# Attention and a token mixer on one core: masks of all pairs from batch 1 on added by VectorE, with the scale and the minus sign taken into the masked block

## The chip, the cores and the metric

The kernel runs on one core of a Trainium2 chip. The metric is the device time of one execution in microseconds; a time given for a kernel is the median of its runs. One further execution is taken with the hardware profiler, and every row of a profile shown here comes from such an execution. The engines are called TensorE (PE in the rows; PEld is its weight load), VectorE (DVE), ScalarE (ACT), GpSimd (POOL) and SyncE (SP), whose queue issues the transfers.

## The reference

Batch 8, 8 heads, 576 positions, head dimension 64, model width 512, everything in fp32.

```python
scores = q @ k.T / sqrt(64)                       # per batch and head, 576 x 576
rel    = pos[:, None] - pos[None, :]
plain  = (rel >= 0) & (rel < 32)                  # heads 0 to 3
dil    = (rel >= 0) & (rel < 128) & (rel % 4 == 0)  # heads 4 to 7
scores = where(mask, scores, -1e9);  scores -= max(scores)
attn   = exp(scores) / (sum(exp(scores)) + 1e-9)
x      = concat_heads(attn @ v)                   # 8 x 576 x 512
theta  = x @ w_theta
y      = w_tok_r @ (x * cos(theta)) + w_tok_i @ (x * sin(theta))
u      = x + y
out    = u + relu(u @ w_ch)
```

The host puts the positions of the dilated heads in order of their remainder by 4, so that both masks become a window of 32 positions inside its own stretch. A block of 32 queries then needs 64 keys.

## The kernel before

**The work.** Heads go in pairs, (batch, pair) with pair 0 to 3. For one pair nine blocks of 128 partitions (two heads, two strips of 32 queries) by 64 keys are computed (`scores`, line 547) into PSUM banks of the kind "s", of which there are two: one for blocks 0 to 4, one for blocks 5 to 8. The mask is an additive tile `mskb` of zeros and large negative numbers. It is added in one of two ways, which `on_pe(b, pr)` chooses:

- *On TensorE* (batch 0 and the pairs (1,2), (1,3), (2,0) and (2,1)): a matmul of an identity with the mask opens the accumulation in the bank (`mask_on_pe`, L501) and the scores are added to it. VectorE takes the maximum over the bank (`row_max`, L507) and, from batch 1 on, multiplies it by minus an eighth (L515). ScalarE computes exp(scale x score + bias) from PSUM, block by block, with its sum (L565); the bank is given back only then.
- *On VectorE* (all other pairs): the matmuls start the accumulation themselves. One instruction per block (`mask_scores`, L486) adds the mask, writes the sum to SBUF (tile `P`) and keeps the maximum; the bank is given back after it. VectorE multiplies the nine maxima by minus an eighth (L578), and ScalarE computes the exponentials from SBUF in place (L584).

Both ways end alike: the sums are inverted (L587, L588), GpSimd multiplies the exponentials by them (L590), VectorE transposes the blocks (`turn`, L608, eight per pair), TensorE multiplies them with the values (`pv`, L704; the tile va holds keys of blocks 0 to 4, vb those of blocks 5 to 8, vb has one buffer), and ScalarE copies the outcome to x (L664). x is then rounded into `xh` and its rest (L678 to L684), `theta` multiplies it with w_theta (L776, L781), cosine and sine follow (L1302 to L1316 and the transposed tail at L858 and L867), `z` is their product with x (L735, L737), the token mix is `token` (L1373) for batches 0 and 1 and a form with seven products in place of eight (`fast_step`, L1169) from batch 2 on, and `chan` (L1406) multiplies with w_ch. The residuals are L1346 and L1382. In the start-up the weights are unpacked and split as well (st_wtk, st_wch: L400 to L427), and the combined token weights of the seven-product form are built by GpSimd, VectorE and ScalarE (tx, ta to td) and stored (tw_t, L1100).

**The order.** Each engine runs its instructions in the order of the program. The program is written by a planner, the class `Order`: every piece of work is a generator that says before each step which engine it needs and for how long (`yield "DVE", 145 * (g1 - g0)`), or what it waits for. The planner keeps the time at which each engine would be free by these costs and lets the step with the lowest rank start. So a changed cost or a step on another engine reorders everything that is planned beside it, on all engines and on the transfer queue. The start-up (batch 0, the scores of batch 1 and of the pairs (2,0) and (2,1), theta of batch 1) is planned by the ranks of a table; from the token mix of batch 1 on, `steady()` gives TensorE a fixed order, and the others follow due times from it.

## Time and profile before

| | us |
|---|---|
| median of 3 runs (lowest, highest) | 564.9 (564.89, 566.3) |
| the profiled execution | 562.37 |
| its span, first to last instruction | 560.6 |
| TensorE busy / mean granted clock | 530.9 / 0.991 |
| VectorE busy | 434.9 |
| ScalarE busy | 372.4 |
| GpSimd busy | 332.5 |

A row of groups reads: line, engine, operation, output <- inputs with shapes, number of instructions, busy time, mean ns of one, idle time of the engine ahead of them and what ended it. A row of a timeline reads: start, duration, engine, line, operation, and in brackets the idle time ahead of it with the instruction that ended it; x5 at its end means five of a kind together, which overlap. A row of waits reads: who waited for whom, us in total, times, longest. "128*64" in a matmul's row is the part of the array that it uses. L12 is line 12 of the kernel.

### The profile page before, as it was taken

What the parts mean: (1) busy time and instruction counts of PE and PEld (TensorE: products, weight loads), DVE (VectorE), ACT (ScalarE), POOL (GpSimd) and SP (SyncE); (2) the same over time, 40 slices, a digit from 0 to 9 for tenths busy, and PEclk for the clock granted to TensorE, in tenths of its full rate; (3) what the DMA queues carried; (4) which work ended last, traced back from release to release, by engine and by line L of the source; (5) the groups of instructions that cost most, each with busy time, mean ns of one, the idle gap of its engine ahead of it and who ended that gap; (6) DMA issues with size and microseconds to landing.
All of it is one profiled execution on the core that took longest, in us unless ns stands there. A gap on an engine that the chain in (4) does not pass through costs nothing.

```text
span 560.6 us, 14386 instructions
## 1 busy us (share of the span) xinstructions
PE 530.9 (95%) x5320; PEld 481.5 (86%) x5320; DVE 434.9 (78%) x1315; ACT 372.4 (66%) x1033; POOL 332.5 (59%) x351
## 2 busy tenths in 40 slices
PE   4897799889998999999999999999999999999997
PEld 3744689778997899998999899998999899989997
DVE  3889799994687787979897997979797997748322
ACT  1598966868748578487776778487767767567220
POOL 2228858788994274763567374655476375727660
PEclk9999799899999999999999999999999999999999
DMA  8991535832659948995499918993599817690622
GB/s 303 400 390 29 177 108 185 256 118 96 201 200 309 317 162 324 322 263 189 141 363 292 307 44 314 324 279 149 199 341 290 276 63 227 213 279 37 211 92 85
DMA packets 59126, 124.41 MB, mean 222 GB/s; under 512 B 5424, under 2 KB 24624, under 8 KB 58800
## 3 DMA queue, kind: packets, MB, share of 16 engines
q1 hardware_dynamic: 59056, 123.49, 64.8%
q8 instruction: 42, 0.69, 0.5%
q14 instruction: 28, 0.23, 0.1%
HBM read 99.88 MB, written 23.59 MB: 220 GB/s over the span
## 4 chain that ended last, share of the span: by engine, by line
PE 70%; DVE 9%; DMA 9%; POOL 5%; ACT 4%; issue 2%; SPq 1%; DVEq 0%; POOLq 0%
PE c L1406 16%; PE th L776 12%; PE C L1169 9%; PE D L1169 7%; PE A L1169 5%; PE B L1169 4%; PE s L547 4%; PE o L704 4%; PE y L1373 4%; DMA vb<-in_vw_dram 4%; DMA st_wtk<-in_wtk_dram 3%; DVE pt L608 3%; POOL z L737 1%; DMA first_k<-in_kT_dram 1%; PE th L781 1%
## 5 line engine op out<-in xcount | busy, mean ns | idle before, releaser
L608 DVE STREAM_TRANSPOSE pt<-P 32x288 f32<-32x288 f32 x224 | 105.2, 470 | 11.8 <-POOL P L590 7.3
L1406 PE MATMUL c<-u,late_wc 128*128 128x288 f32 x768 | 108.3, 295 | 0.0
L1406 PEld LDWEIGHTS c<-u,late_wc 128*128 128x128 f32 x768 | 105.6, 188 | 2.6
L584 ACT ACTIVATE P<-P,mx 128x64 f32<-128x64 f32 x216 | 72.3, 336 | 12.7 <-DVE mx L578 12.5
L776 PE MATMUL th<-wthh,xh 128*128 128x512 f32 x224 | 74.9, 395 | 0.0
L590 POOL TENSOR_TENSOR P<-P,sm 128x576 f32<-128x576 f32 x32 | 39.5, 1235 | 59.0 <-DVE mx L578 29.4
L1187 POOL TENSOR_TENSOR u<-x,u 128x288 fp32r<-128x288 f32 x48 | 40.1, 838 | 20.8 <-ACT u L1185 20.6
L1185 ACT CAST u<-x 128x288 fp32r<-128x288 f32 x48 | 20.5, 427 | 45.0 <-DVE x L1195 45.0
L776 PEld LDWEIGHTS th<-wthh,xh 128*128 128x128 f32 x224 | 42.1, 188 | 9.2
L776 PE MATMUL th<-wthl,xh 128*128 128x512 f32 x112 | 44.3, 396 | 0.0
L486 DVE CUSTOM_DVE_ANT_0 P<-s,mskb 128x64 f32<-128x64 f32 x216 | 33.2, 217 | 14.3 <-PE s L547 14.3
L584 ACT ACTIVATION_READ_ACCUMULATOR P<-P,mx 128x1 f32 x216 | 40.4, 187 | 0.0
L664 ACT COPY x<-o 128x576 f32<-128x576 f32 x32 | 29.5, 921 | 15.0 <-PE o L704 14.9
L737 POOL TENSOR_TENSOR zl<-g,zh 128x512 fp32r<-128x512 f32 x7 | 9.1, 1297 | 48.9 <-ACT zh L735 48.9
L1382 DVE SCALAR_TENSOR_TENSOR x<-c,x 128x288 f32<-128x288 f32 x64 | 28.3, 449 | 12.3 <-PE c L1406 12.2
L547 PE MATMUL s<-k,q 128*64 128x64 f32 x1008 | 36.6, 226 | 0.0
L547 PEld LDWEIGHTS s<-k,q 128*64 128x64 f32 x1008 | 32.8, 140 | 3.7 <-issue 2.7
L704 PEld LDWEIGHTS o<-pt,va 128*64 128x64 f32 x600 | 21.4, 140 | 7.2 <-issue 4.9
L949 POOL TENSOR_TENSOR s<-f,x 128x256 f32<-128x256 f32 x24 | 17.8, 740 | 16.1 <-DVE f L937 13.7
L704 PE MATMUL o<-pt,va 128*64 128x64 f32 x600 | 25.6, 230 | 1.7 <-ACT pt L622 1.2
L1373 PE MATMUL y<-wt_g,z 128*128 128x288 f32 x96 | 20.7, 320 | 6.7 <-POOL z L737 4.1
L776 PEld LDWEIGHTS th<-wthl,xh 128*128 128x128 f32 x112 | 21.0, 188 | 4.0
(245 smaller groups left out, 1609.4 us busy)
## 6 DMA issues: line engine op xcount, KB each, us to landing
q<-in_qT_dram SPq DMA_DIRECT2D x32, 576.0 KB, 5.8
late_wt_a<-tw_t SPq DMA_DIRECT2D x24, 576.0 KB, 6.2
wt_g<-tw_b SPq DMA_DIRECT2D x22, 576.0 KB, 6.1
va<-in_vw_dram SPq DMA_DIRECT2D x30, 320.0 KB, 5.6
k<-in_kT_dram SPq DMA_DIRECT2D x28, 304.0 KB, 6.0
out_dram<-x SPq DMA_DIRECT2D x28, 288.0 KB, 2.1
vb<-in_vw_dram SPq DMA_DIRECT2D x29, 256.0 KB, 4.5
xd<-xq SPq DMA_DIRECT2D x24, 288.0 KB, 5.3
```

Source lines behind the costliest of these rows:

```text
L486: pin(nc.vector.tensor_tensor_reduce(out=P[:, n], in0=ps[:, n - g0], in1=mskb[:, mask_of(pr, n)], op0=ALU.add, op1=ALU.max, scale=1.0, sca ...
L547: pe(nc.tensor.matmul(ps[64 * e:64 * e + 64, n - g0], q[:, qb], k[:, QB * qb:QB * qb + BW], start=not masked, stop=not masked or n == g1 - 1))
L584: table(nc.scalar.activation(P[:, n], P[:, n], AF.Exp, bias=mx[:, n:n + 1], scale=SCALE, accum_out=sm[:, n:n + 1]))
L590: pin(nc.gpsimd.tensor_tensor(P, P, sm.unsqueeze(2).to_broadcast([128, NJ, BW]), op=ALU.mult))
L608: pin(nc.vector.transpose(pmats[b, pr][k0:k0 + QB, :, hh, QB * e:QB * e + QB], P[p0:p0 + QB, :, QB * o:QB * o + QB]))
L664: pin(nc.scalar.copy(dst, src))
L704: pe(nc.tensor.matmul(ps[64 * hh:64 * hh + 64, BW * j:BW * j + BW], v[:, 64 * hh:64 * hh + 64], pmats[b, pr][:, j, hh], start=True, stop=T ...
L776: pe(nc.tensor.matmul(pt, l, r, start=(n == 0), stop=(n == 3 * NC - 1)))
L1169: pe(nc.tensor.matmul(ps, l, r, start=first and n == 1, stop=last and n == 3 * len(ks), skip_group_check=more))
L1187: pin(nc.gpsimd.tensor_tensor(ul[b, d][:, ts], x[:, ts], uh[b, d][:, ts].bitcast(F32), op=ALU.subtract))
L1373: pe(nc.tensor.matmul(ps, l[:, cs], r, start=(n == 0), stop=(n == 3 * NK - 1)))
L1406: pe(nc.tensor.matmul(ps, l[:, cs], r[:, ts], start=(n == 0), stop=(n == 3 * NC - 1)))
```

## The change

Two edits. First, the masked block is no longer plain score plus mask with a running maximum: it is scaled by minus an eighth, and its minimum is kept. Minus an eighth times the maximum is the minimum of the scaled values, so the kept value is the bias of the exponentials, the multiplication L578 goes (24 times), and the exponentials take a scale of minus one. Second, `on_pe` is true for batch 0 alone: the pairs (1,2), (1,3), (2,0) and (2,1) get their masks on VectorE, as all later pairs have them. L501, L507, L515 and L565 run for batch 0 alone or, as L515 and L565, not at all. From line 578 on the changed kernel's lines have numbers lower by 2 (L608 becomes L606, L704 becomes L702, L1373 becomes L1371).

```diff
--- before.py
+++ after.py
@@ -485,12 +485,12 @@
         for n in range(g0, g1):
             pin(nc.vector.tensor_tensor_reduce(
                 out=P[:, n], in0=ps[:, n - g0], in1=mskb[:, mask_of(pr, n)],
-                op0=ALU.add, op1=ALU.max, scale=1.0, scalar=-3e38, accum_out=mx[:, n:n + 1]))
+                op0=ALU.add, op1=ALU.min, scale=-SCALE, scalar=3e38, accum_out=mx[:, n:n + 1]))
         give(*rel)
         signal(key)
 
     def on_pe(b, pr):
-        return b == 0 or (b, pr) in ((1, 2), (1, 3), (2, 0), (2, 1))
+        return b == 0
 
     def mask_on_pe(ps, pr, g0, g1):
         n = g0
@@ -574,14 +574,12 @@
             yield "DVE", dve(S)
             pin(nc.vector.tensor_reduce(sm, P, op=ALU.add, axis=mybir.AxisListType.X))
         elif not on_pe(b, pr):
-            yield "DVE", 67
-            pin(nc.vector.tensor_scalar(mx, mx, -SCALE, None, op0=ALU.mult))
             if b == 1:
                 yield None, "sin0"
             for n0 in range(0, NJ, 3):
                 yield "EXP", 1000 if od.steady else 720
                 for n in range(n0, n0 + 3):
-                    table(nc.scalar.activation(P[:, n], P[:, n], AF.Exp, bias=mx[:, n:n + 1], scale=SCALE,
+                    table(nc.scalar.activation(P[:, n], P[:, n], AF.Exp, bias=mx[:, n:n + 1], scale=-1.0,
                                                accum_out=sm[:, n:n + 1]))
         yield "DVE", 200
         pin(nc.vector.tensor_scalar(sm, sm, 1e-9, None, op0=ALU.add))
```

In the order of the program TensorE loses 24 mask matmuls with their loads, VectorE's rows go from 1214 to 1233. In the steady part TensorE's order is the same row for row; in the start-up the planner puts much in another order. Three places follow. Names are those of tiles with a number behind; s_1_0 is the bank of pair 1 that starts at block 0, y_d_g a token group, o_n the value product of pair n.

*TensorE, around the value product of pair 2 of batch 1 (o_2), inside the token mix of batch 0.* Before:

```order
L1373 MATMUL y_1_1_1167<-late_wt_a,z_0_605 128x288 x3
L1373 MATMUL y_1_1_1167<-late_wt_b,z_4_571 128x288 x3
L1373 MATMUL y_1_1_1167<-late_wt_a,z_1_656 128x288 x3
L501 LDWEIGHTS ids
L501 MATMUL s_0_0_1156<-mskb,ids 128x64
L501 LDWEIGHTS ids
L501 MATMUL s_0_0_1156<-mskb,ids 128x256
L1373 MATMUL y_1_1_1167<-late_wt_b,z_5_637 128x288 x3
L547 MATMUL s_0_0_1156<-k_0_958,q_0_957 64x64 x10
L1373 MATMUL y_1_1_1167<-late_wt_a,z_2_702 128x288 x3
L704 MATMUL o_2_1172<-pt_108,va_2_982 64x64 x10
L704 MATMUL o_2_1172<-pt_108,vb_2_1097 64x64 x8
```

After:

```order
L1371 MATMUL y_1_1_1165<-late_wt_a,z_0_605 128x288 x3
L702 MATMUL o_2_1140<-pt_108,va_2_961 64x64 x10
L702 MATMUL o_2_1140<-pt_108,vb_2_1077 64x64 x8
L1371 MATMUL y_1_1_1165<-late_wt_b,z_4_571 128x288 x3
L547 MATMUL s_0_0_1144<-k_0_932,q_0_931 64x64 x10
L1371 MATMUL y_1_1_1165<-late_wt_a,z_1_656 128x288 x3
```

The value product o_2 stood behind five of the nine rows of token group y_1_1 (a row of x3 is one key tile) and the scores of pair (2,0); it now stands behind one of them. o_3 moves in the same way, ahead of the scores of the pair (2,1).

*VectorE, around the rounding of x for pair 2 of batch 1 (xh_2), from which theta of batch 1 is multiplied.* Before (P_0, and mx_1, s_1, are of the pairs (2,0) and (2,1); pt_108 and pt_110 are the two tiles of transposed exponentials):

```order
L507 TENSOR_REDUCE mx_1_1272<-s_1_5_1346 128x4
L608 STREAM_TRANSPOSE pt_108<-P_0_1153 32x9x32 x2
L515 TENSOR_SCALAR mx_1_1272<-mx_1_1272 128x4
L608 STREAM_TRANSPOSE pt_108<-P_0_1153 32x9x32 x2
L682 TENSOR_TENSOR xh_2_1381<-x_2_1171,xh_2_1381 128x64
L684 TENSOR_TENSOR xh_2_1381<-x_2_1171,xh_2_1381 128x512
L1346 TENSOR_TENSOR x_3_477<-y_3_1_1387,x_3_477 128x288
```

After:

```order
L486 ISA mx_1_1275 128x1
L486 ISA P_1_1274,mx_1_1275<-s_1_5_1337,mskb 128x64
L486 ISA mx_1_1275 128x1
L1344 TENSOR_TENSOR x_2_408<-y_2_1_1285,x_2_408 128x288
L606 STREAM_TRANSPOSE pt_108<-P_0_1141 32x9x32 x2
L680 TENSOR_TENSOR xh_2_1383<-x_2_1139,xh_2_1383 128x64
L606 STREAM_TRANSPOSE pt_108<-P_0_1141 32x9x32 x2
L682 TENSOR_TENSOR xh_2_1383<-x_2_1139,xh_2_1383 128x512
L606 STREAM_TRANSPOSE pt_108<-P_0_1141 32x9x32 x2
```

Four pairs of transposes of P_0 stood ahead of xh_2's L684; now three do, and the fourth stands behind it. Somewhat later on VectorE, where theta's first tile (number 4) is turned by the transposed tail, before:

```order
L1309 SCALAR_TENSOR_TENSOR K_4_1487<-g_4_1488,K_4_1487 64x512
L1382 SCALAR_TENSOR_TENSOR x_1_351<-c_1_0_1509,x_1_351 128x288
L608 STREAM_TRANSPOSE pt_110<-P_1_1271 32x9x32 x2
L858 TENSOR_TENSOR g_4_1488<-xn_4_1489,g_4_1488 64x512
L608 STREAM_TRANSPOSE pt_110<-P_1_1271 32x9x32 x4
L858 TENSOR_TENSOR g_4_1488<-xn_4_1489,K_4_1487 64x512
```

After:

```order
L1307 SCALAR_TENSOR_TENSOR K_4_1479<-g_4_1480,K_4_1479 64x512
L606 STREAM_TRANSPOSE pt_110<-P_1_1274 32x9x32 x2
L1380 SCALAR_TENSOR_TENSOR x_1_351<-c_1_0_1507,x_1_351 128x288
L856 TENSOR_TENSOR g_4_1480<-xn_4_1481,g_4_1480 64x512
L606 STREAM_TRANSPOSE pt_110<-P_1_1274 32x9x32 x2
L856 TENSOR_TENSOR g_4_1480<-xn_4_1481,K_4_1479 64x512
```

Between the two additions L858 (now L856) of that tile stand two transposes in place of four; the other two went ahead of the first.

*SyncE's queue, the loads of values.* vb_2 and vb_3 of batch 1, before:

```order
L400 DMA st_wch_1049<-in_wch_dram 128x1024
L400 DMA st_wch_1099<-in_wch_dram 128x1024
L275 DMA k_1_1059<-in_kT_dram 128x608
L287 DMA va_3_1096<-in_vw_dram 128x640
L304 DMA vb_2_1097<-in_vw_dram 128x512
L400 DMA st_wch_1216<-in_wch_dram 128x1024
L400 DMA st_wch_1244<-in_wch_dram 128x1024
L287 DMA va_0_1241<-in_vw_dram 128x640
L304 DMA vb_3_1242<-in_vw_dram 128x512
```

After:

```order
L275 DMA k_1_1011<-in_kT_dram 128x608
L400 DMA st_wch_1044<-in_wch_dram 128x1024
L287 DMA va_3_1076<-in_vw_dram 128x640
L400 DMA st_wch_1085<-in_wch_dram 128x1024
L304 DMA vb_2_1077<-in_vw_dram 128x512
L287 DMA va_0_1191<-in_vw_dram 128x640
L304 DMA vb_3_1192<-in_vw_dram 128x512
L400 DMA st_wch_1200<-in_wch_dram 128x1024
L400 DMA st_wch_1242<-in_wch_dram 128x1024
```

The k tile moves ahead of both weight loads, one of which moves behind va_3; vb_2 stays behind both; va_0 and vb_3 pass the two later weight loads. Somewhat later vb_3 of batch 2, which stood behind the stores of tb, tx, td and ta (tw_t, L1100), passes those of td and ta, and now stands right behind that of tb.

## The prediction

> **What bounds the kernel now.** I read the first part of the page, then one row per stage, then the waits of the engine that is fullest. The busy line (engine, busy us, share of the span, instructions):
>
> ```profile
> PE 530.9 (95%) x5320; PEld 481.5 (86%) x5320; DVE 434.9 (78%) x1315; ACT 372.4 (66%) x1033; POOL 332.5 (59%) x351
> ```
>
> That is an average over stages with different limits. The same by stage (stretch, its length, then busy time of each engine, the granted clock, DMA share, GB/s):
>
> ```profile
> core 0: us, PE busy (x) PEld busy (x) DVE busy (x) ACT busy (x) POOL busy (x), PEclk, DMA share, GB/s
> 185.13:518.76 333.63, 332.31 (x3244) 309.79 (x3243) 278.75 (x910) 234.78 (x663) 192.42 (x211) 1.00 0.71 239
> 75.00:116.00 41.00, 37.15 (x463) 32.66 (x459) 37.60 (x78) 28.42 (x104) 28.28 (x29) 0.96 0.64 209
> 110.00:170.00 60.00, 56.95 (x553) 52.30 (x553) 43.29 (x131) 42.37 (x116) 54.83 (x61) 1.00 0.48 160
> ```
>
> From 185 us on TensorE idles for 333.63 - 332.31 = 1.32 us in all, while VectorE has 54.9 us to spare: there the time is the work on TensorE, which this change leaves alone. Between 75 and 116 us VectorE (37.60 of 41) is a little fuller than TensorE, and TensorE idles for 3.85 us; from 110 to 170 us GpSimd has only 5.17 us left. So a gain must arise before 185 us. TensorE's idle time there, with what ended it:
>
> ```profile
> PE s L501 <- ACT P L565: 3.0, 2, 1.9
> 81.16 0.31 PE L501 MATMUL s<-mskb,ids 128*128 128x64 bf16 x5 [1.04 <-ACT P L565]
> 102.25 0.30 PE L501 MATMUL s<-mskb,ids 128*128 128x64 bf16 x2 [1.92 <-ACT P L565]
> 125.28 0.63 PE L867 MATMUL xn<-ids,x 128*128 128x128 f32 x4 [1.81 <-DVE g L858]
> 172.63 0.69 PE L704 MATMUL o<-pt,vb 128*64 128x64 f32 x16 [2.19 <-DMA vb<-in_vw_dram]
> 102.25:104.00 1.75, 1.75 (x26) 1.47 (x25) 1.75 (x4) 0.27 (x1) 1.17 (x1) 0.78 0.95 368
> 104.00:107.20 3.20, 3.04 (x40) 2.50 (x40) 2.60 (x8) 3.20 (x13) 1.01 (x2) 0.59 0.86 308
> 123.00:127.00 4.00, 2.19 (x16) 1.91 (x15) 3.25 (x7) 1.56 (x4) 2.98 (x4) 1.00 0.00 0
> 170.00:180.00 10.00, 7.81 (x111) 7.60 (x107) 7.34 (x33) 7.25 (x31) 4.31 (x5) 1.00 0.96 322
> ```
>
> The first two waits are the four old mask-on-TensorE pairs themselves: a score bank can't be written again until the exponentials (L565) have read it. Behind the 1.92 us wait the granted clock is 0.78 and then 0.59: 1.75 x 0.22 + 3.20 x 0.41 = 1.7 us of matmul time. Around the waits of 1.81 and 2.19 us it stays at 1.00 (the last two rows).
>
> **The change part by part.** *Part one, scale and minimum.* It removes L578 24 times and the multiplication inside the exponential stays. The rows:
>
> ```profile
> L578 DVE TENSOR_SCALAR mx<-mx x24: 111/172/773, 59.6 to 467.2; 128x9 f32<-128x9 f32 x24
> L584 ACT ACTIVATE P<-P,mx 128x64 f32<-128x64 f32 x216 | 72.3, 336 | 12.7 <-DVE mx L578 12.5
> 291.59 0.21 DVE L486 CUSTOM_DVE_ANT_0 P<-s,mskb 128x64 f32<-128x64 f32 x1
> 291.73 0.08 DVE L486 DVE_READ_ACCUMULATOR2_ANT mx<- 128x1 f32 x1
> 292.98 1.45 DVE L608 STREAM_TRANSPOSE pt<-P 32x288 f32<-32x288 f32 x3
> L1382 DVE SCALAR_TENSOR_TENSOR x<-c,x 128x288 f32<-128x288 f32 x64 | 28.3, 449 | 12.3 <-PE c L1406 12.2
> L1195 DVE TENSOR_TENSOR x<-D,x 128x288 f32<-128x288 f32 x24 | 10.7, 448 | 10.3 <-PE D L1169 10.1
> ```
>
> In the steady stage 18 times some 0.17 us leave an engine with 54.9 us of room and a chain (mask, exponential, divide, transpose) that TensorE does not wait for: worth 0, and 18 x 0.17 = 3.1 us at most if that cover were gone. Does the masked block get dearer with a real scale and a minimum in place of a scale of one and a maximum? A block starts 0.144 us after the last, and nine take 292.98 - 291.59 = 1.39 us. The trace has no such form; the bounds are 0.144 us (a second operation in the same pass is free) and 0.288 us (a second pass). I take 0.144, since of two operations of one size the one with two arithmetic steps takes 449 ns and that with one 448.
>
> *Part two, four pairs leave TensorE's masks.* Per pair VectorE loses two reductions (L507) and two small multiplications (L515) and gets nine masked blocks. From 80.07 to 115.80 us, VectorE's time in L515 and then in L507, with L515 alone over the run and its worst cases:
>
> ```profile
> 80.07:115.80 35.73, 3.77 (x7) 0.95 0.68 224
> 80.07:115.80 35.73, 2.68 (x6) 0.95 0.68 224
> 83.46 1.30 DVE L515 TENSOR_SCALAR mx<-mx 128x5 f32<-128x5 f32 x1
> 83.29 1.45 POOL L427 TENSOR_TENSOR late_wt_b<-st_wtk,late_wt_b 128x576 fp32r<-128x576 f32 x1 [0.77 <-ACT late_wt_b L425]
> 112.89 0.17 DVE L515 TENSOR_SCALAR mx<-mx 128x4 f32<-128x4 f32 x1
> ```
>
> L515 is 0.17 us when alone and 1.30 when it starts inside GpSimd's subtraction, ending with it (84.76 and 84.74): 3.77 - 7 x 0.17 = 2.6 us of the 3.77 are waiting. Three of the four pairs lie in this stretch: 3.77 + 2.68 = 6.45 us leave, 3 x 1.39 = 4.17 us come, **2.28 us less** on the fullest engine. The fourth, (1,2), lies ahead of it, in a stretch in which VectorE idles for 2.2 of 10 us:
>
> ```profile
> 60.00:70.00 10.00, 6.26 (x34) 5.71 (x31) 7.80 (x32) 9.97 (x43) 8.39 (x8) 0.83 0.40 146
> ```
>
> The Trainium skill, "SBUF — State Buffer", section "Who interferes with whom", says that VectorE and GpSimd share one pair of ports under an exclusive lock, which a VectorE instruction takes when both inputs are in SBUF or in a fast two-port mode, as tensor_scalar may be. The two rows at 83 us agree; the masked block, with one input in PSUM, would be free of it by that rule. By the rule the waiting would pass to the next VectorE instruction of that kind, which is the second rival below.
>
> The order also moves one pair of transposes behind the rounding of x for the third head pair (xh_2), from which theta of batch 1 starts:
>
> ```profile
> 113.09 0.96 DVE L608 STREAM_TRANSPOSE pt<-P 32x288 f32<-32x288 f32 x2
> 114.81 0.68 DVE L684 TENSOR_TENSOR xh<-x,xh 128x512 fp32r<-128x512 f32 x1
> 121.78 0.69 DVE L858 TENSOR_TENSOR g<-xn,g 64x512 f32<-64x512 f32 x1
> 122.50 1.93 DVE L608 STREAM_TRANSPOSE pt<-P 32x288 f32<-32x288 f32 x4
> 124.45 0.68 DVE L858 TENSOR_TENSOR g<-xn,K 64x512 f32<-64x512 f32 x1
> ```
>
> That is another 0.96 us, so xh_2, done at 115.41, could come 3.24 us earlier. Against it stand new waits of VectorE for scores, which now must be written before it can mask (bounds 0, and the 1.04 us of TensorE's first wait put on VectorE instead): I take 0.7. **Term one: -2.5 us.** Between the two additions of theta's first tile (L858, at 121.78 and 124.45) two transposes stand in place of four, the others go to where VectorE waits, so TensorE's 1.81 us wait for the second shrinks by 1.93 / 2: **term two: -0.95 us.**
>
> *On TensorE* the two bank waits (2.96 us), the clock loss (1.7) and the mask matmuls (L501 from 79.5 to 114.5 us: 1.78 us, overlapping others)
>
> ```profile
> 79.50:114.50 35.00, 1.78 (x15) 0.95 (x15) 0.95 0.70 233
> ```
>
> go. None of this is added: TensorE feeds a stage that VectorE sets, and it can't run ahead of VectorE by more than VectorE gains. What is new there: the matmuls with the values (L704 before, o_2 and o_3 of batch 1) are moved ahead of score and token matmuls and wait in order for their transposes and their vb tile; behind them stand the y_1_1 and y_2_1 groups, which residuals on VectorE wait for. As the third pair's value load sits on SyncE's queue thus,
>
> ```profile
> 84.92 2.69 SPq L400 DMA_DIRECT2D st_wch<-in_wch_dram  x2
> 88.69 0.34 SPq L304 DMA_DIRECT2D vb<-in_vw_dram  x1
> vb<-in_vw_dram SPq DMA_DIRECT2D x29, 256.0 KB, 4.5
> 168.52 0.40 SPq L1100 DMA_DIRECT2D tw_t<-td  x1
> 169.01 0.41 SPq L1100 DMA_DIRECT2D tw_t<-ta  x1
> 169.51 0.40 SPq L304 DMA_DIRECT2D vb<-in_vw_dram  x1
> ```
>
> and the new order keeps both weight loads ahead of it (the k tile goes to their front), it lands 4.5 us after 88.7, at 93.2, or some 2 us sooner if the weight tiles come free sooner with VectorE's lead: o_2 can't end before about 91 us. TensorE's lead thus ends in waits of 2 to 3 us at o_2 and o_3: about the size of the two that vanish. The vb tile waited for at 172.63 is issued ahead of the stores of td and ta that it used to follow, 2 x 0.49 = 1.0 us sooner; part of it is spent because TensorE gets there sooner: **term three: -0.2 us**, bounds 0 and -1.0.
>
> *GpSimd* is the lid: from 110 to 170 us it has 5.17 us of room, in an order of its own; a lead of 3.65 us is likely not kept whole. I give back 0.65, bounds 0 and the whole lead. **Sum: -2.5 - 0.95 - 0.2 + 0.65 = -3.0 us.**
>
> The profiled execution took 562.37 us with a span of 560.6, so 1.77 us lie around the span; that gives 559.4. The median of the runs, 564.9, is 2.53 us above the profiled one: 559.4 + 2.5 = **561.9 us**. One measurement of this kernel can tell about 0.3%, 1.7 us, from no change.
>
> **The rivals.** *All of it comes through.* The two bank waits and the clock loss (4.66 us), 0.95 at the theta multiplication and the whole 1.0 at vb: 6.6 us, 558.3. For it: these are TensorE's own idle times and it sets the end. Against: VectorE's gain of 3.2 us bounds the lead.
>
> *The gain doesn't arrive.* The waiting in L515 passes to other VectorE instructions: then the stretch changes by 4.17 - (2.68 + 7 x 0.17) = +0.3 us in place of -2.28, and only the transposes' 0.95 are left, which GpSimd's order takes: about 564.3. For it: L578 swings the same way (111 to 773 ns above). Against: seven chances of colliding vanish and the blocks that come read PSUM.
>
> *Slower: the value matmuls moved ahead become the bound.* Place: o_2 and o_3 in TensorE's queue. Should TensorE stand there for more than the 1.92 us that it stood at 102.25, the clock falls as it did, 1.7 us each time; two such drops and a wait longer by 2 us, less the 3 us gained, is +2.4: 567.3. It decides from the point where the transposes of pair 2, or vb_2, come later than about 91 us. The Trainium skill, "TensorE: Matmul & The Clock Gate", Part 1, section "What's actually happening", has the clock halved after an idle window of about 3.4 us whose phase runs free; the 0.59 after 1.92 us and the full clock after 2.19 us agree only with the free phase, so a wait's length alone would not tell.
>
> *Slower: the masked block needs two passes.* 27 blocks x 0.144 = 3.9 us more in the start-up against a gain of 2.5, and 36 x 0.144 = 5.2 us more per batch on VectorE, whose room is 54.9 us over six batches: at least +1.4, about +5 if half a microsecond per batch finds no cover: 570.
>
> **How the numbers follow.** Chances: forecast 0.45 (561.9; its unknowns move it down by up to 0.7 for the new waits, 0.8 for vb and 0.65 for the lid, and up by 0.3, 0.2 and, for a lid that takes half of the lead, 1.2: its own range is 559.8 to 563.6), all of it 0.10 (558.3), gain that doesn't arrive 0.27 (564.3), moved value matmuls 0.15 (567.3), two passes 0.03. Below 563.2 lie nine tenths of the forecast, all of the second and a tenth of the third with its spread: 0.40 + 0.10 + 0.03 and a little of the waits' rival where its price is small, 0.55. Above 566.6 lie most of the last two and a little of the third: 0.17. The rest, 0.28, is within 0.3%. The range reaches from somewhat below the second case to the fourth, 557.6 to 567.3, leaving out about 0.15.
>
> **What would show it.** Right: row L515 and L578 gone, L486 36 blocks more at 0.14 us each, no TensorE wait for L565 after 75 us, xh_2 (L684 before) done some 2.5 us earlier, the wait at the theta multiplication (L867) under 1 us, and the stretch from then on to the end as long as before. Wrong: a new wait of over 2 us at the value matmuls of batch 1 with a clock under 0.8 behind it; L587 or L417 longer by 2 us in all; GpSimd's work from 110 us on ending when it did; masked blocks of 0.2 us or more apart; or a steady stretch longer than 333.6 us.

## The result and the profile after

The changed kernel takes 561.22 us (median of 5 runs, 560.88 to 563.72), the kernel before beside it 565.6 us (5 runs, 564.89 to 566.3): ratio 0.9933, 95% interval 0.9909 to 0.9957. Once more, with more runs, it took 562.84 us (12 runs) against 565.07 us (34 runs of the kernel before): ratio 0.9971, interval 0.9946 to 0.9997. A ratio is taken over all runs of both kernels and is not the quotient of the two medians. Both intervals hold 0.9946 to 0.9957, a gain of 2.4 to 3.1 us; 561.9 us, 3.0 us less than the 564.9 us known then, was forecast. Chance of the clock explains little of it: the mean granted clock of those 12 and 34 runs is 0.988 and 0.986, and over the runs of one kernel a hundredth of the clock goes with about 1 us (210 runs of all kernels on record), so some 0.2 us.

The first profile of the changed kernel fell on the longest of its five runs (563.72 us, span 562.0), which is longer than the profiled execution of the kernel before (562.37). So two spans can't be compared here, and I took a second profile of each kernel (before: 564.78, span 563.0; change: 562.51, span 560.7). The page of the change, first profile:

```profile
PE 532.8 (95%) x5296; PEld 483.3 (86%) x5296; DVE 440.9 (78%) x1347; ACT 377.4 (67%) x1033; POOL 332.4 (59%) x351
L486 DVE CUSTOM_DVE_ANT_0 P<-s,mskb 128x64 f32<-128x64 f32 x252 | 38.7, 218 | 16.8 <-PE s L547 16.7
L582 ACT ACTIVATE P<-P,mx 128x64 f32<-128x64 f32 x252 | 84.4, 336 | 8.3 <-DVE mx L486 8.1
```

36 masked blocks more, at the mean duration of before (218 against 217 ns): the scale and the minimum cost nothing that shows. On the timeline of VectorE the blocks start 0.14 us apart as they did, but VectorE as a whole is busy 6.0 us more than before (440.9 against 434.9 us):

```profile
291.43 0.21 DVE L486 CUSTOM_DVE_ANT_0 P<-s,mskb 128x64 f32<-128x64 f32 x1
291.57 0.08 DVE L486 DVE_READ_ACCUMULATOR2_ANT mx<- 128x1 f32 x1
291.57 0.22 DVE L486 CUSTOM_DVE_ANT_0 P<-s,mskb 128x64 f32<-128x64 f32 x1
```

For the rest I count from the first matmul of the token mix of batch 0, since no instruction ahead of it differs much between the kernels and yet its start moves from one execution to the next. TensorE's timelines, of before (first and second profile) and of the change (first and second):

```profile
48.66 0.51 PE L1373 MATMUL y<-wt_g,z 128*128 128x288 f32 x2
```

```profile
49.89 0.50 PE L1373 MATMUL y<-wt_g,z 128*128 128x288 f32 x2
```

```profile
49.10 0.51 PE L1371 MATMUL y<-wt_g,z 128*128 128x288 f32 x2
```

```profile
50.77 0.51 PE L1371 MATMUL y<-wt_g,z 128*128 128x288 f32 x2
```

The points below are read on TensorE's timeline, in us after that matmul's start; the wait and the last three rows are durations.

| point on TensorE | before | before, 2nd | change | change, 2nd |
|---|---|---|---|---|
| last token matmul of batch 0 | 63.3 | 62.2 | 63.6 | 65.2 |
| token mix of batch 1 starts | 95.95 | 95.87 | 97.56 | 97.34 |
| wait for the value tile vb_3 of batch 2 | 2.19 | 2.45 | 1.16 | 0 |
| last token matmul of batch 1 | 136.3 | 137.9 | 136.3 | 135.1 |
| first product of batch 2 (A, L1169) | 163.5 | 165.1 | 163.5 | 162.3 |
| from there to the end | 348.4 | 348.0 | 349.3 | 347.6 |
| of it, up to the first product of the last batch | 306.4 | 306.0 | 305.3 | 304.2 |
| of it, from that product to the end | 42.0 | 42.0 | 44.0 | 43.4 |

With the change the token mix of batch 1 starts 1.4 to 1.7 us **later**. What was lost comes back in that mix, and in the second profile more than that; TensorE no longer waits so long there for one value tile. The waits of the changed kernel on TensorE, first profile, and the same places in the second:

```profile
PE o L702 <- DMA vb<-in_vw_dram: 2.8, 5, 1.2
PE c L1404 <- DVE x L1380: 2.6, 1, 2.6
PE o L702 <- DVE pt L606: 2.2, 2, 1.2
PE A L1167 <- DVE x L1380: 1.7, 1, 1.7
```

```profile
94.79 0.80 PE L702 MATMUL o<-pt,va 128*64 128x64 f32 x18 [1.20 <-DVE pt L606]
104.88 1.10 PE L702 MATMUL o<-pt,va 128*64 128x64 f32 x17 [2.83 <-DVE pt L606]
123.48 0.66 PE L1404 MATMUL c<-u,late_wc 128*128 128x288 f32 x3 [1.72 <-DVE x L1380]
173.48 0.69 PE L702 MATMUL o<-pt,vb 128*64 128x64 f32 x16
519.74 0.54 PE L1167 MATMUL A<-wt_g,r1h 128*128 128x288 f32 x2 [1.12 <-DVE x L1380]
```

No matmul waits for a bank held by the exponentials any more. In their place TensorE waits for transposes at o_2 and o_3 (1.20 and 1.00 us in the first profile, 1.20 and 2.83 in the second) and for a residual in the channel product; at vb_3 of batch 2 (173.48) there is no wait in the second profile. The last row is new: in the last batch a first product waits for a residual, 1.74 us in the first profile and 1.12 in the second, and neither profile of the kernel before has a wait there. This is most of the 1.4 to 2.0 us that the last batch takes longer. TensorE's order there is the same; VectorE's is not.

The granted clock behind the 2.83 us (stretch, length, busy times, then the clock as the third number from the end; second profile):

```profile
104.88:106.63 1.75, 1.75 (x34) 1.75 (x34) 1.75 (x4) 0.78 (x2) 0.65 (x1) 0.55 0.91 332
106.63:110.00 3.37, 3.37 (x36) 2.91 (x34) 2.65 (x15) 3.37 (x11) 1.02 (x1) 0.73 0.94 343
```

That is 1.75 x 0.45 + 3.37 x 0.27 = 1.7 us of matmul time, as much as the kernel before lost behind its 1.92 us wait in its first profile.

### The profile page after: what moved, and what is told of

The parts are those of the page before. It is cut to its first block, busy times and chain, and to the rows that moved or that the text cites. A ratio compares the mean times of both kernels' runs of the same rounds, so it can differ in the third digit from the quotient of the medians.

```text
span 562.0 us, 14370 instructions
## 1 busy us (share of the span) xinstructions
PE 532.8 (95%) x5296; PEld 483.3 (86%) x5296; DVE 440.9 (78%) x1347; ACT 377.4 (67%) x1033; POOL 332.4 (59%) x351
## 3 DMA queue, kind: packets, MB, share of 16 engines
q1 hardware_dynamic: 59056, 123.49, 65.2%
## 4 chain that ended last, share of the span: by engine, by line
PE 58%; DVE 15%; POOL 8%; ACT 8%; DMA 7%; issue 3%; SPq 1%; POOLq 0%; DVEq 0%; ACTq 0%
PE c L1404 14%; PE th L774 11%; PE C L1167 7%; PE D L1167 6%; PE A L1167 4%; PE s L547 4%; PE B L1167 4%; PE o L702 3%; DVE pt L606 3%; DMA vb<-in_vw_dram 3%; PE y L1371 2%; ACT P L582 2%; DMA xn<-xd 1%; DVE st_wtk L417 1%; DMA first_k<-in_kT_dram 1%
## 5 line engine op out<-in xcount | busy, mean ns | idle before, releaser
L606 DVE STREAM_TRANSPOSE pt<-P 32x288 f32<-32x288 f32 x224 | 105.1, 469 | 13.0 <-POOL P L588 8.7
L1404 PE MATMUL c<-u,late_wc 128*128 128x288 f32 x768 | 108.5, 296 | 2.6 <-DVE x L1380 2.6
L1404 PEld LDWEIGHTS c<-u,late_wc 128*128 128x128 f32 x768 | 105.5, 188 | 5.4 <-DVE x L1380 2.8
L582 ACT ACTIVATE P<-P,mx 128x64 f32<-128x64 f32 x252 | 84.4, 336 | 8.3 <-DVE mx L486 8.1
L588 POOL TENSOR_TENSOR P<-P,sm 128x576 f32<-128x576 f32 x32 | 37.4, 1168 | 60.7 <-DVE sm L586 53.5
L486 DVE CUSTOM_DVE_ANT_0 P<-s,mskb 128x64 f32<-128x64 f32 x252 | 38.7, 218 | 16.8 <-PE s L547 16.7
L1185 POOL TENSOR_TENSOR u<-x,u 128x288 fp32r<-128x288 f32 x48 | 38.5, 807 | 17.7 <-ACT u L1183 17.4
L582 ACT ACTIVATION_READ_ACCUMULATOR P<-P,mx 128x1 f32 x252 | 47.2, 187 | 0.0
L702 PEld LDWEIGHTS o<-pt,va 128*64 128x64 f32 x600 | 20.6, 137 | 9.3 <-issue 4.4
L702 PE MATMUL o<-pt,va 128*64 128x64 f32 x600 | 25.0, 227 | 3.7 <-DVE pt L606 2.2
L1371 PE MATMUL y<-wt_g,z 128*128 128x288 f32 x96 | 21.5, 329 | 4.9 <-POOL z L735 3.2
```

Source lines behind the costliest of these rows:

```text
L486: pin(nc.vector.tensor_tensor_reduce(out=P[:, n], in0=ps[:, n - g0], in1=mskb[:, mask_of(pr, n)], op0=ALU.add, op1=ALU.min, scale=-SCALE, ...
L582: table(nc.scalar.activation(P[:, n], P[:, n], AF.Exp, bias=mx[:, n:n + 1], scale=-1.0, accum_out=sm[:, n:n + 1]))
L588: pin(nc.gpsimd.tensor_tensor(P, P, sm.unsqueeze(2).to_broadcast([128, NJ, BW]), op=ALU.mult))
L606: pin(nc.vector.transpose(pmats[b, pr][k0:k0 + QB, :, hh, QB * e:QB * e + QB], P[p0:p0 + QB, :, QB * o:QB * o + QB]))
L702: pe(nc.tensor.matmul(ps[64 * hh:64 * hh + 64, BW * j:BW * j + BW], v[:, 64 * hh:64 * hh + 64], pmats[b, pr][:, j, hh], start=True, stop=T ...
L1185: pin(nc.gpsimd.tensor_tensor(ul[b, d][:, ts], x[:, ts], uh[b, d][:, ts].bitcast(F32), op=ALU.subtract))
```

## The experiments

The theory of the prediction (one) puts the gain on VectorE ahead of theta of batch 1. The profiles above made me form theory two: the landing of vb_3 of batch 2 sets when the seven-product form starts. The runs of the experiments came in three groups of four kernels, each group on one chip with its own runs of the kernel before; the "again" runs and the two edits alone are the first group. Of every edit only the lines that matter are shown.

### The kernel before, once more

> The kernel before once more, for a second profile. It should tie with the runs shown: ratio 1.000, inside 0.997 to 1.003. Theory (the gain comes from VectorE's work and TensorE's two waits for the score bank in the start-up): the two waits at the mask matmuls of TensorE (3.0 us in the first profile) are there again, 2.5 to 3.5 us, and the span is within 1 us of 563.5, the typical run's 565.6 less 1.8. Rival (chance of the clock): the waits are small or absent in this profile, and spans of one kernel go up and down with the granted clock by 3 us or more.

565.03 us, ratio 1.002 (0.9996 to 1.0044). The bank waits were there again (0.42 and 2.02 us, a little under the expected sum), the spread too: the first token matmul started at 48.66 and 49.89 us, and at 48.57 to 51.58 us over all kernels of this study. So a difference of less than 3 us between the spans of two profiles says little.

### The changed kernel, once more

> The changed kernel once more, for a second profile: 0.9933 again, within 0.9909 to 0.9957. The first profile of it was a long execution (562.0 us span, clock 0.982, the others 559.0 to 559.9). Theory: a profile of a typical execution has a span near 559.3, theta's first multiplication of batch 1 (first rows of the transposing tail's matmuls) 2 to 3 us sooner than the kernel before, no wait for a score bank, and waits of 1 to 2 us each at the value matmuls o_2 and o_3. Rival (chance of the clock): the start-up is as long as before's and the difference is lost clock alone.

562.84 us, ratio 0.9971 (0.9946 to 0.9997). The ratio missed the expected 0.9909 to 0.9957. No bank wait and the two waits at o_2 and o_3 as the theory said, but theta of batch 1 is not sooner: it starts 64.1 and 65.8 us after the first token matmul in its two profiles, before 64.2 and 63.1.

### The first edit alone

```diff
-        return b == 0
+        return b == 0 or (b, pr) in ((1, 2), (1, 3), (2, 0), (2, 1))
```

(against the changed kernel)

> Only the first edit: scale of minus an eighth and minimum in the masked block, without the multiplication after it; the four pairs keep their masks on TensorE. Theory (the multiplication is off TensorE's path): 0 in the steady stage; the planner shifts the start-up's order, which is worth at most 1 us either way: 565.0, ratio 0.997 to 1.001. The masked block stays 0.144 us from start to start. Rival (the chain mask, exponential, divide, transpose sets the time): 2 to 4 us faster, 562, ratio 0.993 to 0.996. Rival (a second pass): slower by 5 us and blocks 0.288 us apart.

567.26 us, ratio 1.0047 (1.0026 to 1.0068): slower than the theory's range, and not by a second pass (the masked block's mean duration is 216 ns here). TensorE's timeline shows where: without the 67 ns that the planner charged, its order has a run of channel products (L1404) ahead of theta, and they wait in order for weights that are not split yet and for a residual:

```profile
116.33 0.53 PE L1404 MATMUL c<-u,late_wc 128*128 128x288 f32 x2 [1.25 <-ACT late_wc L425]
117.70 0.44 PE L1404 MATMUL c<-u,late_wc 128*128 128x288 f32 x1 [0.84 <-POOL late_wc L427]
120.48 1.81 PE L1404 MATMUL c<-u,late_wc 128*128 128x288 f32 x6 [2.34 <-DVE x L1344]
122.08 0.63 PE L779 MATMUL th<-wthh,xh 128*128 128x512 f32 x1
```

Theta starts 71.7 us after the first token matmul in place of 64.2, the token mix of batch 1 at 100.0.

### The second edit alone

```diff
-        return b == 0 or (b, pr) in ((1, 2), (1, 3), (2, 0), (2, 1))
+        return b == 0
```

(against the kernel before)

> Only the second edit: the four pairs get their masks on VectorE, with the multiplication of the nine maxima kept (28 times instead of 24) and a running maximum. Theory: nearly the whole gain, 562.0, ratio 0.991 to 0.996; the four multiplications cost 0.2 to 0.8 us each on VectorE in the start-up, so it may stay 1 us behind the full change. Rival (both edits are needed, as the small multiplication collides with GpSimd as the ones it replaces did): 564.5, ratio 0.997 to 1.000.

563.96 us, ratio 0.9988 (0.997 to 1.0006): no difference that can be told; the theory had 0.991 to 0.996, its rival 0.997 to 1.000. Its order, too, has channel products ahead of theta (70.7), and the token mix of batch 1 starts at 99.6. In this order, moving four masks to VectorE does not pay by itself; in an order without that run of channel products it was not tested alone.

### The kernel before with one value load issued sooner

```diff
+        if (b, pr) == (2, 2):   # in pv, right behind its matmuls
+            early_vb.append(ap.tile([128, NJ - VA, 128], F32, tag="vb", name="vb2_3", bufs=1))
+            pin(nc.sync.dma_start(early_vb[0], vw[2, 3, :, VA:]))
```

> The kernel before with one transfer moved: the load of the value tile vb_3 of batch 2 is issued right behind the last matmul that reads its buffer, five stores sooner on SyncE's queue; the order on every other engine is unchanged. Theory two (formed on the second profiles: the token mix of batch 1 starts no sooner with the change, and TensorE's way from there is set by the landing of this tile, 2.2 to 2.5 us after TensorE asks for it in the kernel before): the wait falls to 0 to 0.3 us and the time by about 2.2 us, to 562.9, ratio 0.994 to 0.998; about as much as the whole change. Theory one (the gain of the change lies on VectorE ahead of theta of batch 1, and this wait is worth 0.2): 564.5 to 565.1, ratio 0.9985 to 1.001.

564.03 us, ratio 0.9972 (0.9952 to 0.9992). SyncE's queue and TensorE in that profile:

```profile
167.60 0.38 SPq L714 DMA_DIRECT2D vb<-in_vw_dram  x1
```

```profile
170.54 0.69 PE L710 MATMUL o<-pt,vb 128*64 128x64 f32 x16 [0.23 <-DMA vb<-in_vw_dram]
```

The wait is 0.23 us in place of 2.19 and 2.45, the last token matmul of batch 1 comes at 134.3 (before 136.3 and 137.9), and moving one transfer, with every other engine's order as it was, is worth 1.6 us by the ratio, 0.5 to 2.7 by its interval. That is in theory two's range, and the wait went as it said; theory one had allowed 1.001 to 0.9985, which the interval still touches. The profile shows the gain up to this point only. From there to the first product of batch 2 it takes 28.2 us instead of 27.2, and from that product to the end 350.1 instead of 348.0 to 348.4, TensorE being idle for 2.8 us instead of 1.2 to 1.3 up to the last batch, all of it for later value tiles. So in this one execution nothing is left of it, and the 1.6 us rest on the runs.

### The changed kernel with the same load sooner, and later

The sooner one is the edit above. The later one:

```diff
+        if (b, pr) == (2, 3):     # the later one: behind the stores of td and ta again
+            late_vb.append([2, vb])
```

> The changed kernel with the same transfer moved, there two stores sooner. Theory two: the wait was 1.16 and 0 us in the two profiles of the changed kernel, so 0 to 1 us less, 562.4, ratio to the kernel before 0.993 to 0.997, and no wait at that tile in the profile. Theory one: the same as the changed kernel, 562.8; the two cannot be told apart here by time, only by the row of the wait.

> The changed kernel with the load of vb_3 of batch 2 put back behind the two stores that it passes with the change (td and ta); nothing else moves on any engine. Theory two (the gain is this tile's landing): 2 x 0.49 = 1.0 us later, the wait of TensorE at that tile 1.0 to 2.2 us instead of 0 to 1.2, the time up by about 1 us on the changed kernel: ratio to the kernel before 0.995 to 0.999. Theory one: as the changed kernel, 0.993 to 0.997; by time alone the two overlap, by the wait they do not.

Sooner: 562.31 us, ratio 0.9929 (0.9904 to 0.9953), no wait at the tile. Later: 564.38 us, ratio 0.9976 (0.9957 to 0.9994), TensorE waits 1.64 us, and the last token matmul of batch 1 comes at 137.0 (135.5 sooner):

```profile
175.44 0.69 PE L707 MATMUL o<-pt,vb 128*64 128x64 f32 x16 [1.64 <-DMA vb<-in_vw_dram]
```

The two intervals do not overlap, which speaks for the place of this one load being worth something on the changed kernel as well; but the two were measured on different chips, each against its own runs of the kernel before. Neither can be told from the changed kernel itself by time.

### The first edit alone in the order of before

```diff
-            yield "DVE", 67
-            pin(nc.vector.tensor_scalar(mx, mx, -SCALE, None, op0=ALU.mult))
+            yield "DVE", 67
```

> The first edit alone once more, but the planner still charges the 67 ns of the removed multiplication: the order of every engine is that of the kernel before, less the 24 multiplications. The first edit alone with a new order took 567.26, ratio 1.0047. If that loss is the order (the channel products moved ahead of theta of batch 1, which starts 7.5 us later): 565.0, ratio 0.998 to 1.001. If it is the new form of the masked block or of the exponentials: 567, ratio 1.003 to 1.006.

563.82 us, ratio 0.9959 (0.9933 to 0.9986), against 1.0047 in the planner's new order: the same instructions on every engine but in another order are some 5 us apart. And the first edit is worth 2.0 us between the medians (0.8 to 3.8 by the interval), where I had given it 0. Its one profile as a whole is no shorter: its points are 95.97, 137.8 and 164.9, and from there 348.0, all as in the second profile of before. But a row of TensorE shows the multiplication. The value products with va in the stretch from the first product of batch 2 to the first of the last batch, and one of them on the timeline (before, and the first edit):

```profile
L704 PE MATMUL o<-pt,va 128*64 128x64 f32 x400 | 16.8, 227 | 0.0
226.57 0.96 PE L704 MATMUL o<-pt,va 128*64 128x64 f32 x20
```

```profile
L703 PE MATMUL o<-pt,va 128*64 128x64 f32 x400 | 16.0, 227 | 0.0
227.97 0.80 PE L703 MATMUL o<-pt,va 128*64 128x64 f32 x20
```

Of the four such products of a batch the third takes 0.92 to 0.96 us before and 0.80 without the multiplication; inside the one shown a weight load waits for a transpose. Over five batches that is about 0.75 us. All four profiles with the multiplication (the two of before, the second edit alone, the value load sooner) have 16.8 or 16.9 us in this row, all nine without it 16.0. The rest of the 2.0 us is not located. What the profile shows besides is VectorE, in the same stretch (before, and the first edit):

```profile
212.19:518.60 306.41, 305.08 (x3056) 285.50 (x3053) 256.48 (x861) 216.70 (x628) 178.65 (x194) 1.00 0.71 238
```

```profile
213.59:519.58 305.99, 304.28 (x3056) 284.72 (x3053) 250.97 (x841) 216.53 (x627) 178.16 (x192) 1.00 0.71 238
```

18 multiplications less, and VectorE is busy for 5.5 us less, 0.3 us for each.

### Both edits with the old charge

```diff
         elif not on_pe(b, pr):
+            yield "DVE", 67
             if b == 1:
```

> Both edits, with the planner still charging the 67 ns: the order of the second edit alone (563.96, ratio 0.9988) without its 28 multiplications. If the multiplications themselves cost time in the start-up: as the full change, 562.8, ratio 0.994 to 0.998. If only the order counts: as the second edit alone, 564, ratio 0.997 to 1.0005, with theta of batch 1 again starting 6 us later than in the full change.

563.93 us, ratio 0.9971 (0.9953 to 0.999). It has the order of the second edit alone; theta starts at 70.8, the token mix of batch 1 at 99.8, and by time it can be told neither from that kernel (0.9988) nor from the full change (0.9971). So this second removal of the multiplications in an unchanged order is worth 1.0 us by the ratios and nothing by the medians: it fits a small gain and does not confirm 2.0 us. With the charge kept the last batch takes 42.0 us here, as before, and no product waits in it; in the five kernels with the planner's order without the charge (the change, the first edit alone, and the three with the change and a load moved) TensorE waits there for 0.5 to 1.7 us.

### The changed kernel with all value loads sooner, and the first edit with them

```diff
+        if 2 * NP + 3 <= b * NP + pr + 1 < B * NP:   # in pv, right behind its matmuls
+            nb, npr = divmod(b * NP + pr + 1, NP)
+            early_vb.append(ap.tile([128, NJ - VA, 128], F32, tag="vb", name=f"vb{nb}_{npr}", bufs=1))
+            pin(nc.sync.dma_start(early_vb[0], vw[nb, npr, :, VA:]))
```

> The changed kernel with every load of vb from batch 2's last pair on issued right behind the matmuls that read the buffer last. In the steady stage TensorE waits for vb once a batch: 2.93 and 1.12 us in all in the two profiles of the changed kernel, waits for other engines included. If the place on SyncE's queue sets these waits: 1 to 2 us less than the changed kernel, ratio to the kernel before 0.990 to 0.995. If the transfers are late because the transfer engines are full then (share 0.7): the changed kernel's time, or up to 1 us more, since weight loads now wait behind them.

> The first edit alone in the order of the kernel before, which starts the token mix of batch 1 1.6 us sooner than the full change, with all the loads of vb early as in the run beside it. Theory two: the wait at vb_3 of batch 2 (2.0 to 2.5 us in this order) goes, 2 us less than the same kernel without it (563.8): 562, ratio 0.990 to 0.995, as good as the full change without any mask moved to VectorE. Theory one (moving the masks is what pays): no better than 0.996.

562.81 us, ratio 0.9949 (0.9931 to 0.9968), and 561.75 us, ratio 0.9945 (0.9919 to 0.9971). In the steady stage the first still waits for vb once for 1.02 us and once for 0.18, the second 0.76, 0.20 and 0.67: moving the loads up the queue did not take these waits away. The 2.93 and 1.12 us of the expectation were misread: only 1.19 and 0 of them were for vb, the rest was the one wait for a residual in the last batch. The second kernel is the more telling: with every mask of the four pairs left on TensorE, its bank wait of 2.02 us and all, but no multiplication and the tile in time, the kernel is as fast as the full change, as far as 7 runs tell. No version is shown to beat the full change.

### The multiplication doubled

```diff
             pin(nc.vector.tensor_scalar(mx, mx, -SCALE, None, op0=ALU.mult))
+            pin(nc.vector.tensor_scalar(mx, mx, 1.0, None, op0=ALU.mult))
```

> The kernel before with the multiplication of the nine maxima done twice (the second by one), in the same order on every engine. Without the multiplications, in that order, the time was 2.0 us less (0.9959, interval 0.9933 to 0.9986), though 18 of 24 lie in a stage where VectorE has 55 us to spare and no row of the profile shows the gain. If they do set the time: 2 us more, ratio 1.002 to 1.006. If the 2.0 us were the spread between loads of a program: a tie, 0.998 to 1.002.

572.41 us, ratio 1.0115 (1.0087 to 1.0143): 6.5 us slower, more than either expectation. VectorE's groups in the steady stretch, before and doubled (L578 the old, L579 the new one):

```profile
L578 DVE TENSOR_SCALAR mx<-mx 128x9 f32<-128x9 f32 x18 | 5.2, 289 | 0.3
L684 DVE TENSOR_TENSOR xh<-x,xh 128x512 fp32r<-128x512 f32 x15 | 11.5, 764 | 0.0
```

```profile
L578 DVE TENSOR_SCALAR mx<-mx 128x9 f32<-128x9 f32 x18 | 9.3, 518 | 0.3
L579 DVE TENSOR_SCALAR mx<-mx 128x9 f32<-128x9 f32 x18 | 3.1, 174 | 0.6
L685 DVE TENSOR_TENSOR xh<-x,xh 128x512 fp32r<-128x512 f32 x15 | 16.3, 1086 | 0.0
217.44:528.97 311.53, 307.61 (x3057) 286.02 (x3053) 265.65 (x877) 216.18 (x627) 176.16 (x192) 1.00 0.70 233
```

VectorE is busy 9.2 us more for 18 instructions, only 3.1 of which are the new ones' own time: the old ones take 518 ns in place of 289 (4.1 us), and the roundings of x take 1086 in place of 764 (4.8 us); other rows get shorter. The stretch is 5.1 us longer (311.53 against 306.41), though VectorE still has 45.9 us of it free. TensorE's groups, before and doubled, tell where it comes through (the before row of L704 stands above):

```profile
L547 PE MATMUL s<-k,q 128*64 128x64 f32 x616 | 21.2, 223 | 0.0
L1169 PE MATMUL A<-wt_g,r1h 128*128 128x288 f32 x80 | 16.8, 301 | 0.0
```

```profile
L547 PE MATMUL s<-k,q 128*64 128x64 f32 x616 | 22.2, 223 | 1.7 <-DVE x L1383 1.7
L705 PE MATMUL o<-pt,va 128*64 128x64 f32 x400 | 17.2, 227 | 0.4 <-DVE pt L609 0.3
L1170 PE MATMUL A<-wt_g,r1h 128*128 128x288 f32 x81 | 17.6, 306 | 0.0
```

The scores now wait for a residual (L1383, which reads and frees a bank), the value products for transposes, and these groups are spread over 1.0, 0.4 and 0.5 us more (the last row has one record more at the end of the stretch, 0.3 us). These 1.9 us and the rise of TensorE's idle time, 3.92 against 1.33 us, make up 4.5 of the 5.1 us.

## Why the prediction was right, and where it was wrong

**The time and the sign** held: 561.2 and 562.8 us against 561.9, forecast range 557.6 to 567.3. **The working behind them did not hold**, and the number came out by luck: terms one and two, 3.45 us together, did not arrive, while part one and term three, taken at 0 and -0.2 us, were worth about 2.0 and 1.6 us in experiments of their own.

**Part one, "worth 0"**, is the first step that failed. Taken away in an unchanged order the multiplications are worth 2.0 us (0.8 to 3.8) in one order and no more than can be told from nothing in the other; a second set of them costs 6.5 (4.9 to 8.1). Room in a stretch is an average. The chain of mask, exponential, divide and transpose was taken to be one "that TensorE does not wait for", and the third value product of each batch does wait for it: 0.75 us of the gain is that row. The price was mis-sized as well: 0.17 us was the duration when alone, 0.289 the mean in the steady stage, 0.518 with a second one behind it. That removing and doubling are so unequal suggests cover that is nearly used up; it is not shown, since the doubling also lengthens the roundings of x.

**Price of the masked block**: 0.144 us in the new form, as taken; the rival of two passes is out.

**Term one, -2.5 us for VectorE ahead of theta**, is the second step that failed, though not on VectorE. The large piece of xh_2 (L684, now L682) starts 66.15 and 66.08 us after the first token matmul before, and 64.84 and 65.46 with the change: 0.6 to 1.3 us sooner. But theta starts with a tile of 64 positions, which reads the small piece, 128x64 (L682, now L680), and before the change TensorE waits for just this piece. TensorE before, first and second profile:

```profile
114.94 0.49 PE L781 MATMUL th<-wthh,xh 128*128 128x512 f32 x1 [0.72 <-DVE xh L682]
116.10 0.50 PE L781 MATMUL th<-wthh,xh 128*128 128x512 f32 x1 [1.79 <-DVE xh L682]
```

The small pieces of xh_2 on VectorE and of xh_3 on GpSimd, before, and then the change (first profiles):

```profile
114.09 0.80 DVE L682 TENSOR_TENSOR xh<-x,xh 128x64 fp32r<-128x64 f32 x1
113.24 0.32 POOL L682 TENSOR_TENSOR xh<-x,xh 128x64 fp32r<-128x64 f32 x1 [0.30 <-ACT xh L678]
```

```profile
112.57 0.37 DVE L680 TENSOR_TENSOR xh<-x,xh 128x64 fp32r<-128x64 f32 x1
114.50 0.32 POOL L680 TENSOR_TENSOR xh<-x,xh 128x64 fp32r<-128x64 f32 x1 [0.76 <-ACT xh L676]
```

Counted from the first token matmul, the piece on VectorE is done at 66.2 before and at 63.8 with the change (66.2 and 64.5 in the second profiles): 2.4 and 1.7 us sooner, near the forecast, and TensorE no longer waits for it. **What failed is that it sets theta.** The sum followed one of four inputs. The fourth, xh_3, is rounded on GpSimd, and there the piece is done at 65.7 and 66.4 instead of 64.9, and the large one starts at 65.68 and 66.32 instead of 64.87 and 64.81. In the second profile TensorE itself comes to theta only at 65.8, after its wait and lost clock at o_3. The first tile's last matmul is done 1.0 us sooner in the first profile and 0.6 us later in the second, and the first addition on theta's result (L1304, now L1302) is 1.2 and 1.9 us later. Why was not isolated; the chain of waits of the change leads from a weight split on GpSimd (L427) over ScalarE's cast and the exponentials of the moved pairs to the rounding of xh_3, and from there over GpSimd's multiplication of the exponentials (L588) and a pair of transposes to that addition.

Of what L515 wasted, part moved on as the second rival had it; "L587 or L417 longer by 2 us in all" was named as a sign of being wrong, and it came. VectorE's groups from 60 to 118 us, before, and then the change (first profile):

```profile
L417 DVE SCALAR_TENSOR_TENSOR st_wtk<-st_wtk 128x576 uint32<-128x576 uint32 (+1 forms) x5 | 3.8, 794 | 0.0
L417 DVE SCALAR_TENSOR_TENSOR st_wch<-st_wch 128x512 uint32<-128x512 uint32 x4 | 3.8, 940 | 0.4 <-ACT st_wch L415 0.3
L587 DVE TENSOR_SCALAR sm<-sm 128x9 f32<-128x9 f32 x6 | 1.4, 228 | 1.5 <-ACT P L584 1.2 <-ACT P L565 0.3
```

```profile
L417 DVE SCALAR_TENSOR_TENSOR st_wtk<-st_wtk 128x576 uint32<-128x576 uint32 (+1 forms) x5 | 5.1, 1034 | 0.7 <-ACT st_wtk L415 0.7
L417 DVE SCALAR_TENSOR_TENSOR st_wch<-st_wch 128x512 uint32<-128x512 uint32 x4 | 4.5, 1123 | 0.5 <-ACT st_wch L415 0.5
L585 DVE TENSOR_SCALAR sm<-sm 128x9 f32<-128x9 f32 x6 | 1.7, 284 | 3.6 <-ACT P L582 3.5
```

The unpackings L417 take 2.0 us more for the same nine instructions (1.7 in the second profiles), and VectorE waits 2.1 us longer for exponentials, which nothing in the sum had. The longest of the nine with the change takes 1.70 us; a GpSimd subtraction (L427) had started 0.39 us ahead of it and ended 0.32 us ahead of its end. The Trainium skill, "SBUF — State Buffer", section "Who interferes with whom", names just such instructions, with two inputs in SBUF, as those that contend with a GpSimd instruction that reads SBUF; the longer L417 agrees with it, and so does the masked block, whose mean stayed at 216 to 219 ns.

**Term two, -0.95 us at the theta multiplication**: the 1.81 us wait is gone (0 and 0.49 us), but 2.57 and 1.72 us at the channel product ahead of it took its place. Nothing was left of the term.

**Term three, -0.2 us for vb_3 of batch 2**, was named and placed rightly, but mis-sized: the wait went from 2.19 and 2.45 us to 1.16 and 0, which is 1.0 to 2.45 us less and at or beyond the bound of -1.0. It is the largest gain at one place in the profiles of the full change, and its own experiment (2 us less wait on the kernel before, 1.6 us of time) speaks for it.

**The waits at o_2 and o_3, "about the size of the two that vanish"**: 2.2 and 4.0 us for transposes against 3.0 and 2.4 for the banks. The first profile is as forecast; in the second the slower rival's mechanism is there in full, a wait of 2.83 us with clocks of 0.55 and 0.73 behind it, which the prediction had named as a sign of being wrong. The clock loss that was to go is therefore not gone: the change shows it behind o_3 in its second profile, while the second profile of before, with a wait of 2.02 us, shows none (1.00 from 89.89 to 113.89 us). **The lid on GpSimd** was not tested by itself.

**The last batch** is in no term: the full change loses 1.4 to 2.0 us there, with a new wait of 1.74 and 1.12 us.

**What stays open**: averaged over two profiles each and counted from the first token matmul, the full change gains 1.4 us up to the first product of batch 2 and 1.4 us from there to the last batch, of which 0.75 us are the value products, and it loses 1.7 us in the last batch. That is 1.1 us; the time says 2.4 to 3.1. From the first product of batch 2 to the end the two profiles of the change lie 1.7 us apart, so two profiles can't close this gap. What share moving the masks has is open too, since a kernel without it, the first edit with the value loads sooner, is as fast.

## What to carry to other kernels

Cost a small instruction by the chain it stands in and by its mean under load, not by the free time of its engine; doubling it is a cheap way to learn that it costs something, though not how much its removal gives (here 6.5 us against 2.0). Where a planner orders the program, try an edit once in the old order as well: the same instructions lay 5 us apart in two orders. When an engine gets ahead, look at every input of what waits for it, since another one may come last. And anchor profiles at a common instruction before comparing them.

## What the runs showed that was not expected

- A 128x9 multiplication of 0.17 us, added 24 times on an engine with 54.9 us of room in the steady stage, costs 6.5 us, and with it the same instruction ahead of it lasts 518 ns in place of 289.
- The same first instructions reach the first token matmul between 48.57 and 51.58 us after the span's start: a spread of 3 us, of which two profiles of one kernel, the change, show 1.7.
- One value tile of 256 KB, vb_3 of batch 2, landed 2.7 to 4.5 us after its issue over the profiles of all kernels (2.7 with the load later, 4.5 in the first profile of the change). There the issue at 168.49 was followed by TensorE's matmul at 173.07, after a wait of 1.16 us.
